# Batch 0 of a fused attention and FFN kernel: K projected twice, Q by chunk, FFN from single chunks, kv in two pieces, and a new written-out order

## Chip, cores, metric

One core of one Trainium2 chip. The metric is device microseconds (us) of one execution of the program. A core has TensorE (PE, matmul), VectorE (DVE), ScalarE (ACT), GpSimd (POOL) and SyncE (SP); each runs its own instruction queue in order and waits on semaphores. PE writes to PSUM, which has eight banks of 128 x 512 fp32 here. DVE and ACT take results out of the banks. DMAs are issued from the queues of SP, ACT and POOL.

## The reference

8 batches, 8 heads, 576 tokens, head size 64, 128 features. Linear attention with an exponential feature map, then a gated FFN (512 to 1536 to 512) over all 4608 tokens:

```
def phi(x):
    proj = np.einsum('bhsd,df->bhsf', x, w_phi)
    proj = proj - np.max(np.abs(proj), axis=-1, keepdims=True)
    return np.concatenate([np.exp(proj), np.exp(-proj)], axis=-1)
q_p, k_p = (phi(q), phi(k))
kv  = np.einsum('bhsf,bhsd->bhfd', k_p, v)
z   = np.sum(k_p, axis=2)
num = np.einsum('bhsf,bhfd->bhsd', q_p, kv)
den = np.einsum('bhsf,bhf->bhs', q_p, z)[..., None] + 1e-06
x   = (num / den) as rows of 8 heads x 64          # 4608 x 512
out = (np.maximum(x @ w_gate, 0.0) * (x @ w_val)) @ w_out
```

## The kernel before

The program is made of 1427 small steps ("atoms"), each a few instructions of one or two engines. The builder adds them with a key, and a string `ORDER` lists their numbers in the order in which their instructions enter the queues. A number with a prime takes the step's other engine (`copy_of`, line 276): a copy on DVE instead of ACT or the reverse, a scaling on DVE instead of POOL. `z3` and `z1` are matmuls of zeros that keep PE busy. Nothing else sets the order of the work; the queues wait on one another only where data or a buffer is needed. PSUM banks come from one pool of eight (line 172).

**K and V of a batch** (`k_atoms`, `k_item`). Batches 0 and 1 are handled in groups of 4 or 8 blocks of 128 tokens (`K_CUTS`; six groups in batch 0, of 4, 4, 8, 8, 8, 4 blocks, two heads sharing a block's 128 columns as two "parities"). For a group, PE turns K (`kT`, line 271), DVE or ACT copies it out (`kTc`, line 284), PE projects it with `w_phi` into two banks, one for each parity (`kr`, line 312). From these banks DVE takes the maximum of the absolute value (`km`, line 319) and ACT the two exponentials of projection and negated projection (`ke`, line 368). The maximum is not subtracted in the exponent: V's rows are scaled with its exponentials instead (`kk` on ACT, line 379, and `vs` on POOL, line 328). PE then sums K' times V (`kv`, lines 509 and 486), and the result is copied out (`kvc`, line 422). From batch 2 on, K and Q are turned by DMA transposes on SP (`turn`, lines 292 and 298), and tokens 512 to 575 of two batches together form "tails" (tiles km, vm, qm; a load of them is two DMAs, line 236).

**Q of a batch** (`q_item`), in two pairs of chunks; a chunk is 128 tokens. PE projects Q two ways: with features down the partitions (`qc`, line 549), for ACT's exponentials (`qe`, line 567), and with tokens down the partitions (`qr`, line 312), for DVE's maxima (`qm`, line 319). One step `qk` takes the exponentials of all maxima of a pair. Numerator and denominator come from PE (`n`, line 597) and are put together on DVE (`nt`, `nu`, lines 616 and 628, and the reciprocal, line 635); POOL divides (`xu`, line 642). In batches 0 and 1 PE turns the result (`xT`) and a copy writes it into the x of the batch (`xc`, line 662).

**FFN of a batch** (`ffn`). A step takes 128 of the 1536 hidden columns: four matmuls for the value (`fv`, line 734), copied out (line 749); four for the gate (`fg`), joined with the value on DVE (line 756). Then the output in thirds of the hidden columns (`fo`, line 791), copied out (line 805) and stored. Group 8 is the tails. In batch 0 the first four column blocks are done in halves of 256 tokens (`FIRST`, line 20), chunks 0 and 1, then 2 and 3, and the other eight over all 512 tokens.

**Loads.** V in fp32 and the K of batch 0 (fp32, in V's buffer `vn1`, which V of batch 1 takes next) go by SP; everything that is cast on the way (Q, other K, weights) goes by POOL. A small copy on POOL (`gate`, line 831) makes POOL's first load wait for a first piece of K. In the order before, SP's queue reads: loads of K and V of batch 0 (lines 812 to 823, ahead of the list), transposition of qm0 (position 100), V of batch 1 (151), transposition of K of batch 2 (227), and so on. POOL's loads are, in order: q0, k1, wv0, wg0, q1, wv1, qm0, wg1, wv2, wg2, k2, wo (a number after k, v, q is the batch; after wv and wg the third of the columns; after km, vm, qm the pair of batches).

Of the kernel before, what the change touches and what calls it, by code (L numbers as in the profile page):

```python
# [16 lines left out]

K_CUTS = [[4, 8, 16, 24, 32], [8, 16, 24, 32]]

FIRST = ((0, 2, 0, 4), (2, 4, 0, 4), (0, 4, 4, 12))  # L20
# [3 lines left out]


ORDER = """7 z3 82 92 93 83' 84 87 94 86 8 0 98 102 85 89 90 91 88 103 z1 104 96 97 108 105 95 107 106 z1 112
113 109 99 101 110' 111 122 114 115 123' 124 127 118 116 132 1 117 133 119 120 121 125 100' 128 z1
148 149 129 126 187 10 134 188 151 153 155 137 2 131 156 135 158 160 142 130 196 144 136 200 198
150 154 236 139 141 237 143 140 246 247 157 159 152 29 161 162 226 190 192 54 138 256 257 175 163
194 176 164 165 189 145 147' 191 266 177 146 3 267 193 4 169 170 166 167 171 168 195 199 181 178  # L30
182 321 214 5 172 179 183 180 184 201 197 217 215 11 220 221 218 222 219 208 9 322' 216 173 174'
282 283 223 209 185 186' 202 203 238 227' 210 205 206 204 207 240 211 1092 1093 1094 224 225' 239
1095 1096 324 328 228 229 242 212 213' 1097 326 232 1098 1099 1100 1101 1102' 231 6 1103 1104 1105
1106 1107 230 241 1108 243 268 269 270 271 273 258 274 272 261 248 251 260 249 253 255 254 1109 252
259 263 39 1110' 1111 1112' 264 1113 1114 275 250 233 1115 1116' 1117 290 361 262 363 265 292 365
279 280' 281' 323 327 291 295 293 1118 1119 294 1120' 1121 284 325 288 330 30 51 332 334 234 245
244 235 276 277 329 333 285 287 13 40 278' 289 1122 1123 351 296 1124 335 352 353 309 312 310 311
# [3 lines left out]
347' 32 55 61 371 372 307 308' 16 1134 63 388 398 402 399 391 400 383 385 1135' 1136 389 1137 401  # L41
42 403 1138' 405 393 367 368 369 395 392 394 390 1139 1140 1141 33 1142' 1143 1144' 17 43 424 426
428 384 418 454 458 420 1145 456 1146' 422 1147 1148 460 462 464 465 419 421 423 508 512 509 1149
# [4 lines left out]
502 1163 1164 1165' 534 536 538 564 529 531 523 1166 1167 568 503 570 476 574 566 533 569 571 1168  # L48
573 515 514 516 572 18 1169 1170 535 517 539 528 537 530 488 491 524 492 525 526 527 532 1171' 1172
# [70 lines left out]
def kernel(  # L120
# [161 lines left out]
    def turned_copy(st, n, by):  # L282
        st["T"] = sb_T.tile([P, n, P], BF16, name=f"tT{n}", bufs=3 if n == 4 else 2)
        copy_by(by)(st["T"].rearrange("p a b -> p (a b)"), st["pt"][:, 0 : n * P])

    for b in range(TURN, B):
        for n in "kq":

            @atoms.add("turn", n, b)
# [16 lines left out]
    def half_rows(par):  # L306
        return slice(D * par, D * (par + 1))
# [556 lines left out]
```

## Time and profile before

Three runs: 378.77, 378.97 and 380.34 us, median 378.97. One execution was profiled; its first to last instruction are the span. Its own time is not listed apart from the three.

| | |
|---|---|
| median of the runs | 378.97 us |
| span of the profiled execution | 377.4 us |
| PE / DVE / ACT / POOL busy | 98 / 77 / 56 / 40 % |
| granted clock of PE, mean | 0.995 |
| DMA bytes, mean rate | 45.10 MB, 120 GB/s |
| PE matmuls of the FFN, lines 734 and 791 | 1340 of 3502 |

How to read it: busy counts an instruction from start to end, and a matmul's end is modelled, so a busy PE need not be at its peak. Where PE has a steady gap between starts, the count of instructions by that gap is the work. "The chain of waits" follows back from the last instruction to whatever released each step; an engine's idle time matters only where this chain passes through it. A group of instructions carries its line, its engine, its operands as out<-in, shape, count, busy time and the mean of one. In the timeline, neighbours of one kind are merged, and a merged length runs from the first start to the last end. DMA rows give the size and the time from issue to landing. In the profile q0 is `qn`, K of batch 0 and V of batches 0 and 1 are `vn`, and qm0 is `qm`.

### The profile page before, as it was taken

The numbers are of one execution on the slowest core, as the hardware profiler recorded it, in microseconds if no ns is written. First come the engines' busy times: TensorE is split into PE (matmuls) and PEld (weight loads), VectorE is DVE, ScalarE is ACT, GpSimd is POOL, SyncE is SP. The second block draws the span as 40 slices with busy tenths as digits, with TensorE's granted clock in tenths as the row PEclk, the third lists the DMA queues.
The fourth block names the chain that finished last, engine by engine and source line by source line (L and its number), as shares of the span: only waits on it lengthen the run. The fifth ranks groups of instructions, "written<-read, shape, count | busy, mean of one in ns | idle before, by whom it ended". The sixth has DMA issues, their size and how long they took to land.

```text
span 377.4 us, 8960 instructions
## 1 busy us (share of the span) xinstructions
PE 368.1 (98%) x3502; PEld 197.4 (52%) x3502; DVE 290.7 (77%) x633; ACT 213.1 (56%) x509; POOL 151.3 (40%) x201
## 2 busy tenths in 40 slices
PE   7789999999999999999999999999999999999996
PEld 4568465546545555464554554465455444444443
DVE  6998999988876799888868886988768927824641
ACT  6997888877687556876765359882740302111101
POOL 5883672488275275901842126933700210000000
PEclk9899999999999999999999999999999999999999
DMA  8999999999489959781289678620410130021004
GB/s 260 205 200 215 233 131 174 219 172 137 89 213 236 165 67 171 144 182 28 59 160 179 96 174 132 130 16 16 128 41 2 29 113 29 2 67 58 2 2 109
DMA packets 87929, 45.10 MB, mean 120 GB/s; under 512 B 55824, under 2 KB 82000, under 8 KB 87888
## 3 DMA queue, kind: packets, MB, share of 16 engines
q1 hardware_dynamic: 60208, 30.42, 37.3%
q0 software_dynamic: 27200, 13.57, 28.8%
q8 instruction: 27, 0.44, 0.5%
q10 hardware_dynamic: 480, 0.56, 0.5%
q14 instruction: 14, 0.11, 0.1%
HBM read 37.78 MB, written 9.44 MB: 125 GB/s over the span
## 4 chain that ended last, share of the span: by engine, by line
PE 92%; ACT 3%; DMA 3%; issue 0%; SPq 0%; DVE 0%; POOL 0%; DVEq 0%
PE pa L734 49%; PE pa L791 25%; PE pa L597 5%; PE pa L312 5%; PE pa L486 4%; PE pa L549 2%; DMA qn<-in_q_dram 2%; ACT qp L567 2%; PE pa L271 1%; PE pa L509 1%; DMA vn<-in_k_dram 1%; ACT kp L368 1%; ACT kv L422 0%; ACT val_sb L749 0%; ACT xT L662 0%
## 5 line engine op out<-in xcount | busy, mean ns | idle before, releaser
L791 PE MATMUL pa<-wo_sb,h 128*128 128x512 bf16 (+2 forms) x444 | 99.9, 373 | 0.0
L734 PE MATMUL pa<-xT,wv_sb 128*128 128x512 bf16 (+1 forms) x400 | 99.3, 370 | 0.1
L734 PE MATMUL pa<-xT,wg_sb 128*128 128x512 bf16 (+1 forms) x400 | 99.3, 370 | 0.0
L756 DVE SCALAR_TENSOR_TENSOR h<-pa,val_sb 128x512 bf16<-128x512 f32 (+1 forms) x112 | 74.6, 669 | 27.2 <-PE pa L734 20.5
L749 ACT CAST val_sb<-pa 128x512 bf16<-128x512 f32 (+1 forms) x67 | 38.1, 575 | 97.1 <-PE pa L734 88.0
L567 ACT ACTIVATE qp<-pa 128x512 bf16<-128x512 f32 x144 | 76.2, 618 | 15.1 <-PE pa L549 14.8
L368 ACT ACTIVATE kp<-pa 128x512 bf16<-128x512 f32 (+1 forms) x152 | 77.4, 605 | 11.1 <-PE pa L312 9.8
L328 POOL TENSOR_TENSOR vs<-vn,ek 128x512 bf16<-128x512 f32 (+1 forms) x68 | 67.4, 1005 | 31.1 <-DMA vn<-in_v_dram 15.2
L734 PEld LDWEIGHTS <-wv_sb 128*128 128x128 bf16 x448 | 41.9, 98 | 44.9 <-issue 1.2
L734 PEld LDWEIGHTS <-wg_sb 128*128 128x128 bf16 x448 | 41.6, 98 | 43.5 <-issue 0.7
L791 PEld LDWEIGHTS <-h 128*128 128x128 bf16 x444 | 40.8, 98 | 44.6 <-issue 0.8
L319 DVE TENSOR_REDUCE mq<-pa 128x4 f32<-128x512 f32 x72 | 46.5, 683 | 10.4 <-PE pa L312 10.1
L319 DVE TENSOR_REDUCE mk<-pa 128x4 f32<-128x512 f32 (+1 forms) x76 | 47.8, 653 | 3.9 <-ACT kp L368 2.3
L642 POOL TENSOR_TENSOR xu<-u,r 128x512 bf16<-128x512 f32 x22 | 22.8, 1041 | 67.4 <-DVE r L635 53.5
L642 POOL TENSOR_TENSOR tT<-u,r 128x512 bf16<-128x512 f32 x14 | 14.6, 1042 | 73.0 <-DVE r L635 41.0
L628 DVE TENSOR_TENSOR u<-pa,t 128x195 f32<-128x195 f32 (+3 forms) x120 | 38.2, 333 | 3.3
L616 DVE TENSOR_TENSOR t<-pa,cq 128x195 f32<-128x195 f32 (+3 forms) x120 | 36.8, 325 | 2.2 <-PE pa L597 1.0
L597 PEld LDWEIGHTS <-qp 128*128 128x128 bf16 x640 | 28.1, 98 | 14.0 <-ACT qp L567 0.9
L749 DVE CAST val_sb<-pa 128x512 bf16<-128x512 f32 (+1 forms) x45 | 30.7, 682 | 4.5 <-PE pa L734 3.0
L597 PE MATMUL pa<-kv,qp 128*128 128x65 bf16 x640 | 31.0, 193 | 0.9 <-ACT qp L567 0.5
L805 DVE COPY out_sb<-pa 128x512 f32<-128x512 f32 x13 | 8.9, 688 | 13.8 <-PE pa L791 13.6
L486 PEld LDWEIGHTS <-kp 128*128 128x128 bf16 x480 | 16.6, 98 | 3.9 <-issue 0.7
(71 smaller groups left out, 278.4 us busy)
## 6 DMA issues: line engine op xcount, KB each, us to landing
vn<-in_v_dram SPq DMA_DIRECT2D x6, 1024.0 KB, 7.3
qn<-in_q_dram POOLq DMA_DIRECT2D x8, 512.0 KB, 8.6
out_dram<-tT SPq DMA_DIRECT2D x16, 256.0 KB, 2.9
out_dram<-out_sb SPq DMA_DIRECT2D x16, 256.0 KB, 2.9
kn<-in_k_dram POOLq DMA_DIRECT2D x6, 512.0 KB, 9.1
wv_sb<-in_moe_w_val_dram POOLq DMA_DIRECT2D x3, 512.0 KB, 10.2
wg_sb<-in_moe_w_gate_dram POOLq DMA_DIRECT2D x3, 512.0 KB, 9.1
wo_sb<-in_moe_w_out_dram POOLq DMA_DIRECT2D x1, 1536.0 KB, 19.5
```

The lines of the kernel that those rows point to most:

```text
L319: nc.vector.tensor_reduce(m, some.rearrange("p (c f) -> p c f", f=F), axis=AX.X, op=ALU.max, apply_absolute_value=True,)
L328: eng.tensor_tensor(dst[:, :, s, 0:D], src, ek[:, :, s : s + 1].to_broadcast(list(src.shape)), op=ALU.mult,)
L368: nc.scalar.activation(st["kp"][:, s, 0 : n // 2, par, :], st["banks"][par][:, 0 : n // 2 * F].rearrange("p (a f) -> p a f", f=F), AF.Exp, ...
L567: nc.scalar.activation(x["qp"][:, s, slot].rearrange("p a b -> p (a b)"), st["cols", i][par], AF.Exp, scale=sign,)
L597: nc.tensor.matmul(pn[:, E * (2 * i + s) : E * (2 * i + s + 1)], lhsT=x["qp"][:, s, slot, blk, :], rhs=kv_of(b, lo + i)[:, s, :],)
L616: nc.vector.tensor_tensor(x["t", j][rows, 0:n], ab[:, :, 1], c[:, :, None].to_broadcast([np_, n, E]), op=ALU.mult,)
L628: nc.vector.tensor_tensor(x["u"][rows, lo : lo + n], ab[:, :, 0], x["t", j][rows, 0:n], op=ALU.add)
L642: copy_of(alt, nc.gpsimd, nc.vector).tensor_tensor(x["xu"], x["u"][:, :, 0:D], x["r"].to_broadcast([P, H, D]), op=ALU.mult)
L734: nc.tensor.matmul(ps, lhsT=w[:, dc, P * fi : P * fi + P], rhs=xTs[g][:, dc, lo:hi], start=(dc == 0), stop=(dc == NDC - 1),)
L749: copy_by(copy_of(alt, "ACT", "DVE"))(st["val", n], ps)
L756: nc.vector.scalar_tensor_tensor(st["h2"][:, fi, lo:hi], ps, 0.0, st["val", n], op0=ALU.max, op1=ALU.mult)
L791: nc.tensor.matmul(po, lhsT=st["h2"][:, fi, P * t : P * t + P], rhs=wo_sb[:, fi, c0:c1], start=(fi == 0), stop=(fi == NFC - 1),)
```

## The change

It has five parts in code, all in batch 0, and a new `ORDER` of 1437 steps for the whole program.

1. *K twice.* For the six groups of batch 0 a new step `kx` repeats the projection into two further banks; the maxima are taken from these, the exponentials from the first two.
2. *Q by chunk.* For both pairs of batch 0, `qc`, `qr` and `qk` are split by parity, which here is the chunk: one bank and one chunk at a time.
3. *FFN in smaller token pieces.* `FIRST` becomes 128 tokens for column blocks 0 to 3 in chunk 0 and in chunk 1, 256 tokens for blocks 4 to 7 in chunks 0 and 1 and for 0 to 7 in chunks 2 and 3, and 512 for blocks 8 to 11. A piece of 128 tokens takes four column blocks into one bank, one of 256 tokens two, so every copy out is 512 wide; there are 12 value and 12 gate steps, where there were 16 and 16. Matmuls of batch 0's value and gate: 192, before 128.
4. *kv in two.* For both halves of batch 0, the matmuls of the last four of 18 blocks are a step of their own, after the rest.
5. The choice of two output buffers goes by index instead of by a running count.

There are also switches that are left off (`PLAIN` is empty, `Q_TURN` and `X_TURN` are 2 as `TURN` is).

```diff
-FIRST = ((0, 2, 0, 4), (2, 4, 0, 4), (0, 4, 4, 12))
+FIRST = ((0, 1, 0, 4), (1, 2, 0, 4), (0, 2, 4, 8), (2, 4, 0, 8), (0, 4, 8, 12))
+SPLIT = {(0, 0), (0, 1)}
+KV_LAST = {0: 4}
+TWICE = {(0, 0), (0, 1), (0, 2), (0, 3), (0, 4), (0, 5)}
...
-            st["banks"] = [bank(), bank()]
+            st["banks"] = {par: bank() for par in range(2)}
             rows_of(st["T"], st["banks"])
+        twice = key in TWICE
+        if twice:
+            @atoms.add("kx", *key)
+            def _(alt):
+                st["again"] = {par: bank() for par in range(2)}
+                rows_of(st["T"], st["again"])
...
-                row_max(st["m"][:, par:n:2], st["banks"][par][:, 0 : n // 2 * F])
+                row_max(st["m"][:, par:n:2], st["again" if twice else "banks"][par][:, 0 : n // 2 * F])
...
+        last = [x for x in order if x[2] >= 2 * CP * (part + 1) - KV_LAST.get(b, 0)]
+        order = [x for x in order if x not in last] + last
+        cuts = [0, len(order) - len(last), len(order)]
+        for piece, (lo, hi) in enumerate(zip(cuts, cuts[1:])):
...
+            for pars in ((0,), (1,)) if split else ((0, 1),):
+                at = (i, *pars) if split else (i,)
+                @atoms.add("qc", *key, *at)
...
+                @atoms.add("qr", *key, *at)
...
+        for ci in range(len(chunks) if split else 1):
+            @atoms.add("qk", *key, *((ci,) if split else ()))
...
+        def half_step(fi, nf, w, lo, hi):
+            ps = bank().rearrange("p (f n) -> p f n", f=nf)
+            for i in range(nf):
+                for dc in range(NDC):
+                    nc.tensor.matmul(
+                        ps[:, i],
+                        lhsT=w[:, dc, P * (fi + i) : P * (fi + i + 1)],
+                        rhs=xTs[g][:, dc, lo:hi],
```

The two order strings, written out by their keys (first number batch, then group or pair, and so on):

| queue | before | after |
|---|---|---|
| SP, after the loads of K0 and V0 | turn qm0 (100), v1 (151), turn k2 (227), turn km1 (265), turn q2 (279), turn k3, v2, vm1 | vm1 (64), v1 (143), turn qm0 (179), turn k2 (207), turn km1 (224), v2 (273), turn q2 (288), turn k3 (297) |
| POOL, loads | q0, k1, wv0, wg0, q1, wv1, qm0, wg1, wv2, wg2, k2, wo | qm0, q0, k1, wv0, q1, wv1, wg0, wg1, wv2, wg2, wo, k2, km1 |
| POOL, scalings of V0 | ten of twelve; two on DVE | all twelve, behind the first four loads |
| DVE, up to the first FFN step | maxima and copies of K0, Q0 and part of K1, two scalings of V0, mixed with the numerators of all four chunks | 17 steps of K0 (copies and maxima), then copy of Q, the last K maximum, copy of Q, eight Q maxima with two kv copies and three copies of turned K1, six products and six sums of the numerators of chunks 1 and 0, two reciprocals, the copy of chunk 1's x |
| PE, around Q0 | turning of Q pair 0 (56), of pair 1 (60), last K group (62) | turning of pair 1 (58), of pair 0 (59), kv part 0 (82, 91), last K group (90), kv part 1 (112, 113) |
| first FFN step | column block 0, chunks 0 and 1 (173) | column blocks 0 to 3, chunk 1 (166) |
| first output step of batch 0 | 286 | 302 |

The positions are those in the list. Behind batch 0 the steps are the same as before in another order; output thirds of one batch are mixed with value and gate steps more than before. The last steps of both lists are the last output tile's two parts of 352 and 160 columns.

More of the change, by code (lines that the diff above doesn't have):

```diff
@@ L284, in turned_copy @@
         copy_by(by)(st["T"].rearrange("p a b -> p (a b)"), st["pt"][:, 0 : n * P])
-    for b in range(TURN, B):
-        for n in "kq":
+    for b in range(min(TURN, Q_TURN), B):
+        for n, first in (("k", TURN), ("q", Q_TURN)):
+            if b < first:
+                continue
             @atoms.add("turn", n, b)
@@ L310, in rows_of @@
         for j in range(T.shape[1]):
-            for par in range(2):
+            for par in banks:
                 nc.tensor.matmul(
@@ L751, in _ @@
+        for n, (fi, nf, lo, hi) in enumerate(steps):
+            @atoms.add("fv", g, n)
+            def _(alt, n=n, fi=fi, nf=nf, lo=lo, hi=hi):
+                ps = half_step(fi, nf, wv_sb, lo, hi)
+                st["val", n] = sb_g.tile([P, SF], BF16, name="val_sb")
+                copy_by(copy_of(alt, "ACT", "DVE"))(
+                    st["val", n], ps.rearrange("p f n -> p (f n)")
+                )
             @atoms.add("fg", g, n)
-            def _(alt, n=n, fi=fi, lo=lo, hi=hi):
+            def _(alt, n=n, fi=fi, nf=nf, lo=lo, hi=hi):
```

269 lines of the change are left out of this document (151 added, 118 removed), and 38 rows, old and new, of the table ORDER.

## Prediction

> **What bounds the kernel now.** I read the page first, then the chain of waits in order of time, then busy time by windows, then the queues of SyncE (SP) and GpSimd (POOL).
>
> ```profile
> span 377.4 us, 8960 instructions
> PE 368.1 (98%) x3502; PEld 197.4 (52%) x3502; DVE 290.7 (77%) x633; ACT 213.1 (56%) x509; POOL 151.3 (40%) x201
> PE 92%; ACT 3%; DMA 3%; issue 0%; SPq 0%; DVE 0%; POOL 0%; DVEq 0%
> ```
>
> TensorE (PE) carries 92% of the chain that ended last; the other 8%, some 30 us, is where time can be won or lost. The chain in order of time (start, length, what) says where that is:
>
> ```profile
> 3.79 8.76 DMA qn<-in_q_dram
> 12.60 1.78 PE pa L271 x16
> ...
> 342.62 20.72 PE pa L734 x96
> ```
>
> 96 matmuls in 20.72 us are 0.216 us each, without a gap: late in the program PE works at its rate, and only the amount of work counts. At the start the chain hangs on the load of batch 0's Q (q0 below), which lands at 3.79 + 8.76 = 12.55. Busy time by windows:
>
> ```profile
> core 0: us, PE busy (x) PEld busy (x) DVE busy (x) ACT busy (x) POOL busy (x), PEclk, DMA share, GB/s
> 4.00:12.55 8.55, 6.54 (x51) 3.81 (x49) 6.77 (x13) 7.44 (x25) 5.98 (x11) 1.00 1.17 296
> 12.60:31.00 18.40, 16.60 (x338) 12.76 (x339) 17.63 (x52) 17.49 (x46) 15.90 (x22) 0.91 1.32 203
> 24.00:36.00 12.00, 11.21 (x153) 9.07 (x152) 10.85 (x37) 10.55 (x23) 6.96 (x8) 1.00 1.34 194
> 36.00:48.00 12.00, 12.00 (x124) 6.53 (x123) 10.92 (x20) 9.41 (x30) 6.75 (x11) 1.00 1.22 242
> ```
>
> From 36 us on PE is full (12.00 of 12.00). From 12.6 to 31, VectorE (DVE) and ScalarE (ACT) are full (17.63 and 17.49 of 18.40) and PE waits for them. So the time is the moment at which the FFN can begin to feed PE, plus the PE work that is then left. That moment is the first FFN matmul:
>
> ```profile
> 28.91 0.60 PE L734 MATMUL pa<-xT,wv_sb 128*128 128x256 bf16 x4
> ```
>
> It comes 28.91 - 12.55 = 16.4 us after q0 has landed. The change alters this distance, the landing of q0, and the work that is left.
>
> **Part 1: from q0 to the first FFN.** The new order starts the FFN on one 128-token chunk. I counted what DVE must do, in its new order, from q0's landing to that point: two copies of turned Q, one half-wide K maximum, eight Q maxima, two kv copies, three copies of turned K of batch 1, six products and six sums of the numerators, two reciprocals, one copy of turned x.
>
> ```profile
> L319 DVE TENSOR_REDUCE mq<-pa 128x4 f32<-128x512 f32 x72 | 46.5, 683 | 10.4 <-PE pa L312 10.1
> L662 DVE COPY xT<-pa 128x512 bf16<-128x512 bf16 x1 | 0.4, 427 | 0.2 <-PE pa L271 0.2
> ```
>
> ```profile
> 5.40 0.43 DVE L319 TENSOR_REDUCE mk<-pa 128x2 f32<-128x256 f32 x1 [0.23 <-ACT kp L368]
> 13.99 1.28 DVE L284 COPY tT<-pa 128x1024 bf16<-128x1024 bf16 x2
> 15.80 2.06 ACT L567 ACTIVATE qp<-pa 128x512 bf16<-128x512 f32 x4 [0.41 <-PE pa L549]
> 18.65 0.94 DVE L284 COPY tT<-pa 128x512 bf16<-128x512 bf16 x2
> 19.51 1.88 DVE L319 TENSOR_REDUCE mq<-pa 128x4 f32<-128x512 f32 x3
> 23.16 0.42 DVE L422 CAST kv<-pa 128x260 bf16<-128x260 f32 x1
> 25.09 0.20 DVE L635 RECIPROCAL r<-u 128x8 f32<-128x8 f32 x1
> 26.14 0.79 DVE L616 TENSOR_TENSOR t<-pa,cq 128x195 f32<-128x195 f32 x3
> ```
>
> One maximum lasts 0.683 and three in a row 1.88, so each further one adds (1.88 - 0.68)/2 = 0.60: neighbours overlap by 0.08. With that overlap taken off where it applies: Q copies 1.2; maxima 8 x 0.60 = 4.8, and 0.4 for the half-wide one; kv copies 0.7; K copies 3 x 0.43 = 1.3; twelve numerator steps at 0.79/3 = 0.26, 3.1; reciprocals and x copy 0.8. Sum 12.3. Ahead of it PE turns the first half of Q, half of the 1.78 above, 0.9. So the first FFN comes 13.2 us after q0, against 16.4: **-3.2**. ACT allows it: it has eight pairs of Q exponentials (2.06 for four, so 8.2 in all), two half-wide K pairs and five small steps, about 10.9 behind 2 us of turning and projecting. What makes the distance shorter is work that moves behind the first FFN: by position, 22 numerator matmuls with their DVE steps, and the second chunk's x.
>
> **Part 2: when q0 lands.** Here the order moves DMAs. On POOL, the Q tails of batches 0 and 1 (qm0) are now issued ahead of q0. On SP, batch 0's loads were followed by the transposition of qm0, and batch 1's V (v1) stood behind that. SP's waits and its timeline:
>
> ```profile
> SPq L298 <- DMA qm<-in_q_dram: 23.6, 1, 23.6
> ```
>
> ```profile
> 27.71 1.30 SPq L298 DMA_TRANSPOSE qmT<-qm  x1
> 29.26 0.40 SPq L220 DMA_DIRECT2D vn<-in_v_dram  x1
> ```
>
> SP stood 23.6 us at that one wait, so v1 left at 29.26, although the buffer that it takes (K of batch 0 was in it) was free once PE had turned the last of K0. That was at 11.6:
>
> ```profile
> 3.79 1.07 POOL L214 DMA_DIRECT2D qn<-in_q_dram  x1
> 11.19 0.44 PE L271 MATMUL pa<-ident,vn 128*128 128x128 f32 x2
> 21.24 1.42 POOL L236 DMA_DIRECT2D qm<-in_q_dram  x2
> ```
>
> In the new order SP's queue holds vm1 (V tails of batches 2 and 3), v1, and only then the transposition. vm1 has nothing to wait for and leaves at about 4; v1 leaves after that last turning, near 11. An engine goes by its own queue, not by the position in the list: SP waited from 4 us on, at position 100. So both loads meet q0.
>
> ```profile
> vn<-in_v_dram SPq DMA_DIRECT2D x1, 1152.0 KB, 11.5
> vm<-in_v_dram SPq DMA_DIRECT2D x6, 128.0 KB, 8.4
> qm<-in_q_dram POOLq DMA_DIRECT2D x8, 64.0 KB, 4.1
> ```
>
> ```profile
> 36.00:41.00 5.00, 5.00 (x49) 3.07 (x47) 4.54 (x10) 4.13 (x15) 0.06 (x1) 1.00 1.22 297
> 41.00:46.00 5.00, 5.00 (x25) 2.25 (x23) 4.66 (x8) 3.40 (x12) 4.69 (x8) 1.00 1.24 205
> ```
>
> Bounds for q0: at the least only qm0 is ahead of it, 128 KB at the 203 GB/s that POOL's loads reach by themselves, +0.65: 13.2. At the most vm1 (256 KB) and v1 (1152 KB) pass q0 too, 1.44 MB at the 296 GB/s of that stretch, +4.9 more: 18.1. v1 landed 11.5 after its issue, so at 40.8; while it ran, in 36 to 41, everything together moved 297 GB/s, against 205 after it. 1.18 MB at 297 are 4.0. v1 starts near 12, and by then q0, behind qm0, has hardly begun; most of v1 passes it. I take 17.0, near the upper end, **+4.4**.
>
> The Trainium skill (DMA: Bandwidth & Descriptors, section Where 436 GB/s comes from) gives about 358 GB/s for loads from HBM. By that the 1.44 MB would cost 4.0, an estimate from that page, and the sum would be up to 0.9 lower; the windows here show less than 300, and I stay with them.
>
> Nothing covers this wait. In DVE's queue seventeen steps of K0 stand ahead of the first Q copy, done near 13; behind it stands all of Part 1. In PE's queue the turning of Q stands ahead of the last K group's projection and of kv. POOL could become late as well, since all twelve V scalings are now its own and start 1.42 later:
>
> ```profile
> L328 POOL TENSOR_TENSOR vs<-vn,ek 128x512 bf16<-128x512 f32 (+1 forms) x68 | 67.4, 1005 | 31.1 <-DMA vn<-in_v_dram 15.2 <-ACT ek L379 11.5 <-ACT pa L409 2.6
> ```
>
> 12 x 1.0 and a load's issue from 8 us on end at 21 to 22; kv wants the last of them some 5 us after q0, at 22. That costs nothing with q0 at 17.0, and up to 3 with q0 at 13.2.
>
> First FFN: 17.0 + 13.2 = 30.2, **+1.3**.
>
> **Part 3: PE work that is left then.** It grows, since Part 1 put some of it off. From the chain in order of time:
>
> ```profile
> 34.86 3.64 PE pa L734 x28
> 57.65 0.81 PE pa L597 x26
> 69.35 0.45 PE pa L271 x8
> 84.64 0.78 PE pa L312 x24
> ```
>
> 22 numerators x 0.031 = 0.7, eight turnings (x and K1) 0.45, eight projections of K1 0.26: +1.4. FFN pieces: 64 more matmuls in batch 0. The 28 in 3.64 are 24 of 256 columns and 4 full ones; (3.64 - 4 x 0.216)/24 = 0.116 against half of 0.216, so 0.008 each more: +0.4 to +0.5. The second projection of K, 36 x 0.0325 = 1.2, lies ahead of the first FFN, where PE waits for DVE; without that cover it would cost its 1.2. Fewer and wider copies out of the FFN's banks spare DVE and ACT some 0.6 each, but behind PE: nothing. kv in two pieces adds no matmul. wo's load now stands ahead of K of batch 2, priced at nothing as long as its transposition is done before PE's queue comes to it. Part 3: **+1.8**.
>
> What the second projection buys is small:
>
> ```profile
> DVE mk L319 <- ACT kp L368: 0.2, 1, 0.2
> ```
>
> In the first 36 us DVE waited 0.2 us for ACT on a shared bank. The Trainium skill (PSUM — Partial Sum Buffer, section PSUM bank collisions raise a hardware error) says that two engines must not read one bank at once, so that schedulers order them. By that rule each K maximum stands against its exponentials, and separate banks should win more than 0.2; here other steps of DVE fill those gaps, and the sum by the trace stays.
>
> **Sum**: +1.3 (which is +4.4 - 3.2, with rounding) + 1.8 = +3.1: span 380.5. The median of the three runs, 378.97, lies 1.6 above the span, and I hold that fixed. **Forecast 382.1.**
>
> **The rivals.**
> *The loads do not collide*: v1 shares little, or leaves late. q0 at 13.4, first FFN 26.6: -2.3 + 1.8, so 378.5, no change. For it: q0 was being served when v1 would start. Against it: v1's buffer was free at 11.6 already.
> *Faster*: q0 at 13.2, first FFN 26.4 (-2.5); the 0.8 us that PE lacked in 24 to 36 goes as well, because single chunks reach it more evenly, and of the 1.8 some 1.0 is done there: 376.5. It decides if q0 lands before 13.4 and POOL is in time. Against it: DVE and ACT, full already, have no room.
> *Weights late*: POOL's loads are a queue at 203 GB/s until 31 us, so all slide with q0: K1 19.9, then 2.6 each, Q1 25.1, the third value block 35.5. The transposition of qm0 now shares with them; past 2.5 us of that, the turning of Q1 and the FFN wait: +2.5, 384.6.
> *The second projection does not do what it is for*: that is inside the forecast, 1.2 of PE's waiting time for at most 0.2.
>
> **How the numbers follow.** Collision 0.55, no collision 0.23, faster 0.12, late weights 0.10. A measurement here tells 0.5%, 1.9 us, from no change: faster is below 377.1, slower above 380.9. The collision case goes from q0 at 15.5 (380.6) to 18.1 (383.2), so a tenth of it is no change; a tenth of the second is faster. Faster 0.14, same 0.27, slower 0.59. Range 377.2 to 384.6.
>
> **What would show it.** Right: v1 leaves SP near 11; q0 lands at 16 or later; DVE is idle 3 to 4 us before the first copy of turned Q; the first FFN is near 30 and PE full from about 36. Wrong: q0 before 14.5 (Part 2 fails), more than 14.5 us from q0 to the first FFN (Part 1 fails), or gaps of PE after 40 us, which a new order could hold anywhere and which no row of before can show.

## The result, and the profile after

The changed kernel takes 390.02 us (median of four runs, 388.79 to 393.09) against 379.31 (four runs, 378.77 to 380.34): ratio 1.029, interval 1.0245 to 1.0335, 10.7 us slower. Ratios here and below are of fast executions alone; of the experiments' executions one was slow (392.68 us, before with K0 projected twice). The profiled execution took 389.5. The forecast, 382.1, had the direction; the time lies 5.4 us above the end of its range.

Of the page of the changed kernel: the span, the busy times, the granted clock in 40 slices, and the shares of the chain.

```profile
span 387.7 us, 9067 instructions
PE 372.0 (96%) x3550; PEld 205.9 (53%) x3602; DVE 292.3 (75%) x637; ACT 221.1 (57%) x521; POOL 139.5 (36%) x182
PEclk9788999999999999999999999999999999999999
PE 84%; DMA 6%; DVE 5%; issue 2%; ACT 1%; POOL 0%; SPq 0%; DVEq 0%
```

PE's share of the chain fell from 92% to 84%; transfers, DVE and "issue" took it. 52 matmul records are missing (3550 of 3602, up to five in any 20 us), so gaps of 0.1 to 0.2 us in the PE rows are not evidence here. I use the weight loads (PEld), which are complete. Lines have moved: turning 290, projection by rows 333, numerators 675, value and gate 814, output 875, loads 233 to 271.

The chain of the changed kernel in order of time (start, length, what):

```profile
3.81 1.47 POOL qm L255 x2
5.29 10.20 DMA qn<-in_q_dram
...
15.54 1.90 PE pa L290 x16
...
17.73 11.04 DMA qn<-in_q_dram
...
28.82 2.53 PE pa L290 x22
```

q0 lands at 5.29 + 10.20 = 15.49. The chain then does not go through the steps of DVE, as forecast, but through a second load, that of batch 1's Q (q1). It leaves at 17.73 and lands at 28.77. POOL's timeline says why it leaves then, the DMA rows of the kernel before say what the same load took there, and PE's timeline says when the FFN begins:

```profile
17.73 0.94 POOL L233 DMA_DIRECT2D qn<-in_q_dram  x1 [3.35 <-PE pa L290]
```

```profile
qn<-in_q_dram POOLq DMA_DIRECT2D x1, 512.0 KB, 8.5
```

```profile
32.27 0.94 PE L814 MATMUL pa<-xT,wv_sb 128*128 128x128 bf16 x14
```

q1 takes q0's buffer, so POOL waited 3.35 us until PE had turned q0. The load then took 11.04 us against 8.5. The turning of Q1 (positions 144 and 149) stands ahead of the first FFN step (166) in PE's queue. So the first FFN step comes at 32.27, 16.8 us after q0, 3.4 later than before.

This is one execution. Four of the experiments below have the same loads up to q1, and their profiles show how much q0 varies:

| kernel | q0 lands | q1 lands | first FFN step |
|---|---|---|---|
| after | 15.49 | 28.77 | 32.27 |
| Q1's turning late | 15.37 | 28.23 | 28.86 |
| after, then the later order of before | 16.84 | 29.35 | 31.65 |
| K once | 17.09 | 28.94 | 32.24 |
| V2 late | 18.43 | 29.44 | 32.91 |

With q0 at 16.84 or later the chain runs through q0's load and the steps behind it, as forecast, though more through PE's and ACT's than through DVE's, and the first FFN step comes 14.4 to 15.1 us after PE begins to turn q0. With q0 at 15.49 it runs through q1. The two paths are nearly equally long, and the first FFN step stays between 31.65 and 32.91 unless Q1's turning is moved.

On SP:

```profile
4.07 1.55 SPq L255 DMA_DIRECT2D vm<-in_v_dram  x2
12.03 0.39 SPq L239 DMA_DIRECT2D vn<-in_v_dram  x1
```

The two loads of V left about when the forecast said (4 and near 11). Busy time by windows (columns as in the prediction):

```profile
10.00:20.00 10.00, 7.59 (x87) 5.38 (x86) 7.19 (x14) 6.69 (x19) 6.63 (x11) 0.75 1.30 233
20.00:30.00 10.00, 8.76 (x221) 7.10 (x218) 8.55 (x25) 8.11 (x22) 8.76 (x13) 0.84 1.31 204
30.00:40.00 10.00, 10.00 (x166) 8.92 (x166) 7.84 (x23) 7.20 (x14) 5.54 (x7) 0.89 1.24 207
```

DVE and ACT, full before, are now busy 6.7 to 8.6 of 10. PE's granted clock is 0.75 to 0.89 in these windows; before it is 0.83 from 10 to 20 us and 1.00 from there on. This shows on the path: from 28.8 to 31.3 us the granted clock is 0.50, and the 22 turnings behind q1's landing (last line of the chain above) take 0.115 us each, where eight in the kernel before took 0.45, 0.056 each. So some 1.3 us of the 3.4 are the clock's in this execution.

**Where the 10.3 us of span went.** Take the start of each step's first weight load and subtract the PE work that the list has put ahead of it, each matmul at its duration by shape (0.216 us for 512 columns, 0.031 for a numerator, 0.0325 for a projection, and so on). What remains is the time that PE has lost so far, to waits, to a lower clock and to anything else between its instructions. In us, at seven times (the lower four kernels are experiments, below); next to a long stop a figure can be 1.5 off, since it hangs on the step that is read:

| kernel | 38 | 58 | 70 | 100 | 160 | 290 | 340 | PE work |
|---|---|---|---|---|---|---|---|---|
| before | 14.2 | 14.7 | 15.1 | 15.9 | 17.7 | 20.3 | 20.4 | 355.6 |
| after | 17.5 | 18.1 | 19.7 | 21.6 | 25.0 | 29.4 | 29.5 | 356.7 |
| before, then the later order of after | 14.4 | 15.2 | 15.6 | 17.3 | 20.3 | 24.5 | 24.6 | 355.6 |
| after, early loads as before | 11.6 | 18.8 | 19.9 | 21.7 | 24.9 | 29.4 | 29.4 | 356.7 |
| before, early loads as after | 21.2 | 21.9 | 22.3 | 23.3 | 24.8 | 28.0 | 27.9 | 355.6 |
| before, K0 projected twice | 15.6 | 16.3 | 16.8 | 17.7 | 19.3 | 22.1 | 22.2 | 356.6 |

After less before: 3.4 us up to 58 us, 1.1 of added work, 1.2 more between 58 and 70, and 4.5 spread over all that follows. Together 10.2. More than half of the loss comes behind the place at which the forecast stopped looking for gaps.

Between 58 and 70 there is one stop, 1.4 us at 63.7 (timeline of the changed kernel):

```profile
63.59 0.25 ACT L661 ACTIVATE cq<-mq 128x8 f32<-128x8 f32 x1
65.15 0.38 PE L675 MATMUL pa<-kv,qp 128*128 128x65 bf16 x7 [1.41 <-issue]
65.38 0.56 DVE L694 TENSOR_TENSOR t<-pa,cq 128x130 f32<-128x130 f32 x2 [2.12 <-PE pa L675]
65.62 1.09 ACT L641 ACTIVATE qp<-pa 128x512 bf16<-128x512 f32 x2 [1.78 <-PE pa L675]
```

DVE and ACT wait for PE, and PE for nothing that the profile names ("issue").

### The profile page after: what moved, and what is told of

Its sections match the earlier page's. It is cut to its first block, busy times and chain, and to the rows that moved or that the text cites. A ratio compares the mean times of both kernels' runs of the same rounds, so it can differ in the third digit from the quotient of the medians.

```text
span 387.7 us, 9067 instructions
## 1 busy us (share of the span) xinstructions
PE 372.0 (96%) x3550; PEld 205.9 (53%) x3602; DVE 292.3 (75%) x637; ACT 221.1 (57%) x521; POOL 139.5 (36%) x182
## 4 chain that ended last, share of the span: by engine, by line
PE 84%; DMA 6%; DVE 5%; issue 2%; ACT 1%; POOL 0%; SPq 0%; DVEq 0%
PE pa L814 47%; PE pa L875 21%; DMA qn<-in_q_dram 5%; PE pa L675 5%; PE pa L333 4%; PE pa L548 4%; PE pa L622 2%; PE pa L290 2%; DVE h L838 1%; DVE tT L719 1%; DVE mk L340 1%; DVE t L694 1%; DVE u L706 1%; DMA vn<-in_k_dram 1%; PE pa L580 1%
## 5 line engine op out<-in xcount | busy, mean ns | idle before, releaser
L838 DVE SCALAR_TENSOR_TENSOR h<-pa,val_sb 128x512 bf16<-128x512 f32 x108 | 73.5, 688 | 35.0 <-PE pa L814 33.6
L814 PE MATMUL pa<-xT,wv_sb 128*128 128x512 bf16 (+2 forms) x421 | 93.9, 355 | 0.6
L814 PE MATMUL pa<-xT,wg_sb 128*128 128x512 bf16 (+2 forms) x414 | 92.0, 354 | 1.3 <-ACT qp L641 0.2
L829 ACT CAST val_sb<-pa 128x512 bf16<-128x512 f32 x71 | 41.6, 588 | 87.1 <-PE pa L814 75.9
L349 POOL TENSOR_TENSOR vs<-vn,ek 128x512 bf16<-128x512 f32 (+1 forms) x65 | 65.5, 1017 | 68.0 <-ACT ek L429 56.0
L415 ACT ACTIVATE kp<-pa 128x512 bf16<-128x512 f32 (+1 forms) x152 | 77.0, 590 | 15.9 <-PE pa L333 11.9
L641 ACT ACTIVATE qp<-pa 128x512 bf16<-128x512 f32 x144 | 76.4, 609 | 15.7 <-PE pa L622 13.7
L706 DVE TENSOR_TENSOR u<-pa,t 128x195 f32<-128x195 f32 (+3 forms) x120 | 37.2, 331 | 1.6 <-POOL tT L719 0.2
L719 POOL TENSOR_TENSOR xu<-u,r 128x512 bf16<-128x512 f32 x18 | 19.7, 1100 | 51.8 <-DVE r L713 17.8
L675 PE MATMUL pa<-kv,qp 128*128 128x65 bf16 x640 | 33.0, 194 | 2.2 <-issue 1.4
L829 DVE CAST val_sb<-pa 128x512 bf16<-128x512 f32 x37 | 25.4, 688 | 11.6 <-PE pa L814 11.2
L719 POOL TENSOR_TENSOR tT<-u,r 128x512 bf16<-128x512 f32 x8 | 8.3, 1040 | 42.6 <-DVE r L713 42.6
L889 ACT COPY out_sb<-pa 128x512 f32<-128x512 f32 (+1 forms) x12 | 6.9, 577 | 19.0 <-PE pa L875 19.0
## 6 DMA issues: line engine op xcount, KB each, us to landing
kn<-in_k_dram POOLq DMA_DIRECT2D x6, 512.0 KB, 10.3
```

The lines of the kernel that those rows point to most:

```text
L349: eng.tensor_tensor(dst[:, :, s, 0:D], src, ek[:, :, s : s + 1].to_broadcast(list(src.shape)), op=ALU.mult,)
L415: nc.scalar.activation(st["kp"][:, s, 0 : n // 2, par, :], st["banks"][par][:, 0 : n // 2 * F].rearrange("p (a f) -> p a f", f=F), AF.Exp, ...
L641: nc.scalar.activation(x["qp"][:, s, slot].rearrange("p a b -> p (a b)"), st["cols", i, par], AF.Exp, scale=sign,)
L675: nc.tensor.matmul(pn[:, E * (2 * i + s) : E * (2 * i + s + 1)], lhsT=x["qp"][:, s, slot, blk, :], rhs=kv_of(b, lo + i)[:, s, :],)
L706: nc.vector.tensor_tensor(x["u"][rows, lo : lo + n], ab[:, :, 0], x["t", j][rows, 0:n], op=ALU.add)
L814: nc.tensor.matmul(ps[:, i], lhsT=w[:, dc, P * (fi + i) : P * (fi + i + 1)], rhs=xTs[g][:, dc, lo:hi], start=(dc == 0), stop=(dc == NDC - 1),)
```

## The experiments

In the diffs below a line is a place in the list, by key; where a step changes its function, the code is shown. Each ratio is against runs of the kernel before on the same chip (medians 379.3 to 379.9).

### The two halves of the list

```diff
 ORDER of after, places 0 to 299
-ORDER of after, places 300 to 1440
+the steps that are left, in the order of before
```

> The changed kernel with its own order for the first 300 places (batch 0, the first group of the FFN's steps, up to about 58 us) and, behind them, the order of the kernel before for all that is left. Theory: the loss has two parts. By the weight loads of TensorE, the changed kernel is 3.6 us behind before at 58 us, has 1.1 us more TensorE work, and loses another 5.5 us between 58 us and the end. So this kernel should lose the first two alone: 379.3 + 4.7 = 384 us. Rival: the whole loss comes from the start (late loads, a late first FFN step), and what is lost later follows from it: 389 to 390 us, as the changed kernel.

Measured: 386.38 us, ratio 1.0153 (1.006 to 1.0246, a wide interval: 2.3 to 9.3 us).

```diff
 ORDER of before, places 0 to 283
-ORDER of before, places 284 to 1430
+the steps that are left, in the order of after
```

> The kernel before with its own first 284 places and, behind them, the changed kernel's order for all that is left. K is projected once, Q whole, the FFN by 512 hidden columns, as before. Theory of two parts: it loses only what the later order costs, 379.3 + 5.5 = 385 us, with first FFN step at 29 us as before. Rival, all of the loss from the start: 379 us, within 1 us of before.

Measured: 383.46 us, ratio 1.009 (1.0056 to 1.0125). The two medians add up: +6.7 and +3.8 against +10.7 for both. The rival (all from the start) falls by the second kernel, whose interval excludes no change. My split was 1.5 to 2.4 us off: the start costs more, the later order less. PE's waits from 28 us on, in the second kernel:

```profile
PE pa L734 <- ACT qp L567: 0.2, 1, 0.2
PE pa L734 <- DVE h L756: 0.2, 1, 0.2
PE pa L597 <- DVE mk L319: 0.2, 1, 0.2
PE pa L312 <- DVE kv L422: 0.2, 1, 0.2
```

The same view of before has no line from 36 us on. No single wait makes the later order's loss: by the table it grows from 0.5 us at 70 to 4.2 at 290. What the waits show is 0.8; the rest is spread over steps too short for that view, and its cause stays open. It is not a larger number of changes between matmuls of 64 and of 128 rows: between 70 and 340 us there are 56 of them in before and 57 in this kernel.

### What sets the start: V late, Q1's turning late

```diff
-ld vm1 (64)
-ld v1 (143)
 turn qm0 (179)
+ld vm1
+ld v1
```

> The changed kernel with the two loads of V that left early on SP (the tail rows at 4.07 us, batch 1 at 12.03 us) put back behind the transposition of Q's tail rows, as before. Theory: they share the DMA engines with the loads of Q for batches 0 and 1, which land at 15.49 and 28.77 us; without them q0 lands 1 to 2 us earlier and q1 3 us earlier, the first FFN step comes at 29 to 30 us instead of 32.4, and the time falls by 2 to 3 us, to 387 to 388. Rival: POOL's queue alone sets when q0 and q1 land (qm ahead of q0; K of batch 1 and a third of W_val ahead of q1): they land where they did, 390 us.

Measured: 389.41 us, ratio 1.0235 (1.015 to 1.0319). Its chain:

```profile
5.29 8.94 DMA qn<-in_q_dram
...
16.47 12.67 DMA qn<-in_q_dram
```

q0 lands 1.3 us earlier as expected, but q1 takes 12.67 us and lands at 29.14, as late as ever. The transposition comes early in this kernel too, so V1 left at 14.62, only 2.6 us later, and met q1 instead of q0. Inconclusive for the collision.

```diff
-qT 1 0 (144), qT 1 1 (149), qTc 1 0 (155), qTc 1 1 (161)
 fg 0 0 4 0 1 (202)
+qT 1 0, qTc 1 0, qT 1 1, qTc 1 1
```

> The changed kernel with the two turnings of batch 1's Q and their copies put behind the first six FFN steps in the order, so that TensorE does not wait for q1 (28.77 us) ahead of the first FFN step. Theory: the first FFN step comes 13 to 14 us after q0, at 29 us, and about 2 us of the 3.5 us lost at the start are won back: 388 us. Rival: the first FFN step waits for its own operand (the normalised and turned rows of batch 0) nearly as long as for q1, or the wait turns up again at Q1's projection: within 0.5 us of 390.

Measured: 390.69 us, ratio 1.0265 (1.0177 to 1.0352). In its trace PE turns q0 at 15.41 and the first FFN step comes at 28.86, 13.45 us later: with Q1 out of PE's way the distance is close to the forecast 13.2. Yet nothing is gained. The stop near 63 us is 2.3 us long instead of 1.4, and PE waits elsewhere:

```profile
PE pa L675 <- issue: 2.3, 1, 2.3
PE pa L675 <- DVE mk L340: 0.8, 1, 0.8
...
PE pa L814 <- ACT kp L415: 0.6, 1, 0.6
```

### A buffer of its own for q1

```diff
+def load_q1(b, name, src, eng, dtype):
+    t = sb_in.tile([P, H * C // 2, P], dtype, name="qT1").rearrange("p a b -> p (a b)")
 ...
 ld q0 (24)
+ld q1
 ld k1 (31)
...
-ld q1 (75)
```

> The changed kernel with a buffer of its own for batch 1's Q (the one that batch 3's turned Q takes much later), and its load directly behind batch 0's Q on POOL, instead of at 17.73 us after TensorE has turned batch 0's Q. Theory: batch 1's Q lands near 20 to 21 us instead of 28.77, TensorE no longer stands before its turning, the first FFN step comes 13 to 14 us after q0, at 29 to 30 us instead of 32.4, and, since Q1's own work is not put off as in the kernel with the late turning, the 3 us are kept: 387 us. Rival: the projections and the V scalings of batch 1 are set by K1 and the weights, which now land later; the first FFN step moves little and the time is 389.5 to 391.

Measured: 392.18 us, ratio 1.0338 (1.0297 to 1.0379), the slowest of all by its median. The rival holds: the wait only changes its name. K of batch 1 is now the load that takes long, and the turning of K1 also stands ahead of the first FFN step, which comes at 34.28. From its chain:

```profile
7.75 17.91 DMA kn<-in_k_dram
...
25.70 1.03 PE pa L295 x8
```

### The loads alone, both ways

```diff
 ld wv1 (98)
+ld qm0
...
 turn qm0 (179)
+ld vm1, ld v1
...
 turn k3 (297)
+ld v2
```

> The changed kernel with the order of its loads put back to that of before in four places: Q's tail rows behind the second third of W_val on POOL, the tail rows and batch 1 of V behind the transposition of Q's tail rows on SP, batch 2 of V behind the transposition of batch 3's K. Theory: q0 lands at 12.5 to 13.5 us instead of 15.49 and q1 at 25 to 26 instead of 28.77; first FFN step near 29; the stop of TensorE at 63.7 us goes as well; together 3 + 1.5 us less: 385 to 386 us. What then is left over before (6 us) is the second projection of K, about 1.1 us of TensorE work, and the later order, 3.8 us. Rival: the loads are hidden and the order of the compute steps alone makes the start late: q0 lands earlier but the first FFN step stays at 32 us, 389 to 390 us.

Measured: 388.47 us, ratio 1.0235 (1.0206 to 1.0263), not the 385 to 386 expected. In this kernel PE turns q0 at 12.86 and the first FFN step comes at 26.30, 13.44 us later and 2.6 us earlier than in before. By the table PE has lost 11.6 us at 38 us: 2.6 less than before, 5.9 less than after. Nearly all of it goes again, in one wait of 4.8 us and behind it (from 56.5 to 63.3 us the granted clock is 0.50):

```profile
PE pa L580 <- POOL vs L349: 4.8, 1, 4.8
```

```profile
vn<-in_v_dram SPq DMA_DIRECT2D x1, 1152.0 KB, 18.7
```

V of batch 1, issued at 29.76 with W_out, K2 and Q2 on their way, needs 18.7 us to land; POOL's scalings start at 48.65, and the kv matmuls of batch 1 stand in PE's queue for them. Now the converse, before's compute order with after's loads:

```diff
+ld qm0
 ld q0 (0)
...
+ld vm1, ld v1
 turn qm0 (100)
```

> The kernel before with only its early loads ordered as the change orders them: Q's tail rows ahead of batch 0's Q on POOL, the tail rows and batch 1 of V ahead of the transposition of Q's tail rows on SP. Theory (the forecast's own term): q0 lands at 14 to 17 us instead of 12.55 and the first FFN step as much later; 381 to 383 us. Rival: it lands later, but VectorE and ScalarE use the time for batch 0's K, so that less than half of it stays: 379.5 to 380.5.

Measured: 386.55 us, ratio 1.0183 (1.0158 to 1.0208): **6.9 us for three moved loads**, more than twice what I expected. Its chain and its largest PE wait:

```profile
5.29 10.31 DMA qn<-in_q_dram
15.64 1.90 PE pa L271 x16
17.83 14.12 DMA qn<-in_q_dram
31.99 0.72 PE pa L271 x8
```

```profile
PE pa L271 <- DMA qn<-in_q_dram: 4.1, 1, 4.1
```

q0 is 3 us late; q1, whose buffer q0 holds, leaves 2.5 us later than in before and then takes 14.12 us instead of 8.5.

The leaving matters less than it seems. In the five kernels of the table above and in the one with V late, q1 leaves anywhere between 16.47 and 20.66 and lands between 28.23 and 29.44. An estimate by the bytes ahead of q1 fits better: the three loads are 1536 KB, which at the 204 GB/s of 20 to 30 us in the changed kernel are 7.7 us, and q1 lands 8.2 later than in before (31.95 against 23.75). In the changed kernel the first third of W_gate, 512 KB, stands behind q1 and not ahead of it; the 1024 KB that are left are 5.1 us, and q1 lands 5.0 later. One of the three loads by itself:

```diff
+ld v1
 turn qm0 (100)
...
-ld v1 (151)
```

> The kernel before with one load moved: V of batch 1 stands on SP ahead of the transposition of Q's tail rows, so it leaves near 11 to 12 us instead of 29.26. Q's tail rows stay late on POOL, V's tail rows stay late too. Theory: of the 6.9 us that the changed order of the loads costs on the kernel before, this one megabyte is the larger part: it passes the end of q0's load and the loads in front of batch 1's Q; q0 lands 0.5 to 1.5 us later, q1 at 28 to 30 us instead of 24; 383 to 385 us. Rival: Q's tail rows ahead of q0 are the part that counts, since they put off every later load of POOL's queue, and V1 alone costs 0 to 1 us.

Measured: 382.58 us, ratio 1.0077 (1.0048 to 1.0105). V1 alone costs 3.3 us, just below the theory's range and not the rival's 0 to 1. Its chain goes through q1, which is issued at 15.27 (in before at 15.28) and takes 12.26 us; it lands 3.8 later, where the estimate by bytes would say 5.8:

```profile
15.27 12.26 DMA qn<-in_q_dram
27.58 1.03 PE pa L271 x8
```

If the loads' costs add, the other half, 3.6 us, belongs to Q's and V's tail rows, which were not run by themselves.

### The stop at 63.7 us

```diff
-ld v2 (273)
 turn q2 (288)
 turn k3 (297)
+ld v2
```

> The changed kernel with one load moved: V of batch 2 (1 MB, issued on SP at 56.30 us ahead of the transposition of batch 2's Q) stands behind the transposition of batch 3's K, as in the kernel before. In the changed kernel TensorE stops for 1.4 us at 63.7 us, with nothing that the profile names; the one transfer that ends then is a 16 KB packet of the instruction queue (62.91 to 63.87 us), asked for some 4 us late by the count of TensorE's instructions, while 16 DMA engines were full; the kernels with late V or late turning stop there too (1.4 and 2.3 us). Theory: TensorE ran out of instructions, because the packet stood behind the crowd of V2, K3 and the transposition of Q2; with V2 out of the way it comes near 59 to 60 us, the stop goes, and the time falls by 1.4 to 2 us, to 388 to 388.6. Rival: the stop is a wait for a buffer or a bank that the profile does not name; it stays, 390 us.

Measured: 388.21 us, ratio 1.022 (1.0189 to 1.025), 1.8 us less by the medians; the intervals just touch. PE's waits after 28 us for which the profile names nothing, first of the changed kernel, then of this one, in which the stop is gone:

```profile
PE pa L675 <- issue: 1.4, 1, 1.4
PE pa L875 <- issue: 0.5, 3, 0.2
```

```profile
PE pa L875 <- issue: 0.5, 3, 0.2
```

The page of the changed kernel has a queue for instructions (packets, MB, share):

```profile
q8 instruction: 28, 0.46, 0.5%
```

28 packets of 16 KB for some 7200 instructions of PE (3602 weight loads and as many matmuls) are one for every 256. In the changed kernel the sixth runs from 62.91 to 63.87 us, and PE goes on at 65.15. Count PE's instructions up to the moment this packet has landed, in all kernels with the changed start:

| kernel | landed at | instructions issued by then | stop of PE |
|---|---|---|---|
| after | 63.87 | 1720 | 1.4 |
| V late | 64.85 | 1720 | 1.4 |
| Q1's turning late | 63.46 | 1720 | 2.3 |
| after, then the later order of before | 63.65 | 1720 | 2.2 |
| start kept, below | 60.98 | 1720 | 2.0 |
| own buffer for q1 | 64.87 | 1698 | 0.3 |
| V2 late | 63.01 | 1686 | none |
| K once, below | 64.66 | 1670 | none |
| early loads as before | 60.43 | 1570 | none |
| first of "Can the early start be kept?" | 61.90 | 1670 | none |
| the same, K once | 63.25 | 1632 | none |
| start kept, K once | 61.54 | 1668 | none |

PE stops at exactly 1720 wherever the packet comes later than that, and, but for 0.3 us in one kernel, not where it comes earlier. Instruction 1721 is issued 1.3 to 1.6 us after the landing in all five, and 1.4 after it with the own buffer for q1 and with V2 late, which is why the first of these still stops for 0.3. It is not the step itself, a numerator in every kernel of the table: it passes without a stop where the packet is early. So PE has run out of instructions. Late in the changed kernel the packets leave at 6526, 6792 and 7038 instructions issued, about 256 apart; by that spacing the sixth was due near 1410, and left at 1700. Two things meet there. PE takes instructions fast: it issues number 1406 at 58.7 us and number 1662 at 60.7. And the packet left 4.2 us after number 1406. With V2 out of the way it left 2.7 us after it and landed at 63.01, not at 59 to 60 as expected. That fits a packet held up by the data transfers, of which V2 was a part; what else holds it was not tested. In two of these kernels the view of waits names DVE for the stop ("DVE u L706: 2.2" and "2.0"): DVE had been done, and its semaphore was only the last event seen. The Trainium skill (Runtime: NRT & Kernel Launch, section Instruction fetch mechanics) says that instructions come in 16 KiB blocks through a DMA queue that the sequencer drives, and that the cost is mostly hidden. The block size agrees; here it was not hidden, at 1.4 to 2.3 us.

### The second projection of K

```diff
-TWICE = {(0, 0), (0, 1), (0, 2), (0, 3), (0, 4), (0, 5)}
+TWICE = set()
-kr 0 u, kx 0 u
+kr 0 u, where the first of the two stood
```

> The changed kernel with K of batch 0 projected once, the maxima and the exponentials read from the same banks as before the change; all else, the order too, as changed (a projection stands where the first of its two stood). Theory: the second projection is 36 matmul pairs, 1.2 us of TensorE work in a stretch in which TensorE waits for q0 and q1 anyway: the time falls by 0 to 0.5 us, 389.5 to 390. Rival A: the work is on the path, 388.8. Rival B: with one bank the exponentials of ScalarE and the maxima of VectorE get into each other's way (banks come free later), and the time rises by 0.5 to 1 us.

Measured: 386.49 us, ratio 1.0184 (1.015 to 1.0217), 3.5 us less than after. 1.0 is PE work and 1.4 the stop (the list is 72 instructions shorter, so PE reaches the limit after the packet, as the table shows); about 1 us more is not accounted for. The theory (0 to 0.5 us) falls; it is rival A, the work is on the path, and more. The converse:

```diff
+        if key[0] == 0:
+            @atoms.add("kx", *key)
+            def _(alt):
+                st["again"] = [bank(), bank()]
+                rows_of(st["T"], st["again"])
...
 kr 0 u
+kx 0 u
```

> The kernel before with only the second projection of batch 0's K added, directly behind the first, the maxima read from its banks. Theory: 36 more pairs of 0.033 us, 1.2 us, in a stretch where TensorE waits, and four banks of eight taken at once: 0 to 1 us slower, 379.5 to 380.7. Rival A: VectorE and ScalarE no longer wait for each other at a bank, and the time falls by 0.5 us. Rival B: banks run short ahead of the first FFN step and the time rises by 2 us or more, which would put most of the start's loss on the second projection.

Measured: 381.74 us, ratio 1.0053 (1.0032 to 1.0074): 2 us slower. In its trace PE turns q0 at 13.74 and the first FFN step comes at 31.17, 17.4 us later, where before has 16.3. (That q0 is turned 1.1 later than in before is within what q0 varies as POOL's first load, 12.5 to 13.7.) DVE's waits for PE's projections up to 33 us, first of before, which has one such line, then of this kernel (with its waits for turned tiles, 1.5 us in before):

```profile
DVE mk L319 <- PE pa L312: 0.4, 1, 0.4
```

```profile
DVE mq L319 <- PE pa L312: 2.0, 1, 2.0
DVE tT L284 <- PE pa L271: 1.8, 2, 0.9
DVE mk L319 <- PE pa L312: 1.2, 2, 0.8
```

The maxima now wait for PE, 3.2 us in all against 0.4; the doubled projections stand in PE's queue ahead of what DVE needs next. PE "waiting for DVE" was not free room.

### Can the early start be kept?

```diff
 places 0 to 299 of after, then the order of before
 ld q1
+ld qm0
 turn qm0
+ld v1
 turn k3
+ld v2, ld vm1
```

> The changed kernel's first 300 places with four loads moved (Q's tail rows directly behind batch 1's Q on POOL; batch 1 of V behind the transposition of Q's tail rows; batch 2 of V and the tail rows of V behind the transposition of batch 3's K), and the order of the kernel before for all the rest. In the kernel with the loads as before, TensorE was at 51.9 us 5.7 us ahead of the changed kernel (first FFN step at 26.5 us) and lost it again in one wait of 4.8 us for POOL's scaling of batch 1's V, whose load took 18.7 us to land behind W_out and K2. Theory: with V1 on its way some 5 us earlier that wait goes; first FFN step at 26.5 to 28 us, no stop of TensorE near 63 us, the later order as before: 1 to 2 us faster than before, 377.5 to 379 us. Rival: V1 in flight with Q1 makes Q1 late again, first FFN step at 30 us or later, 380 to 382.

Measured: 384.74 us, ratio 1.0125 (1.0096 to 1.0153). That is neither the theory's 377.5 to 379 nor the rival's 380 to 382: the first FFN step comes at 27.30, but with V1 earlier the weights are late. Chain and waits:

```profile
23.92 17.20 DMA wv_sb<-in_moe_w_val_dram
41.17 6.99 PE pa L814 x36
```

```profile
PE pa L814 <- DMA wv_sb<-in_moe_w_val_dram: 2.6, 1, 2.6
```

The same with one projection of K (`TWICE = set()`, `kr` where the first of the two stood):

> The same, with K of batch 0 projected once, maxima and exponentials read from the same banks. Theory: the 1.0 us of TensorE work of the second projection lies in stretches in which TensorE waits for Q, and only the part that does not costs: within 0.5 us of the kernel with both. Rival A: it is on the path, as the 3.5 us between the changed kernel and the one with a single projection suggest (of which 1.8 us were the stop for instructions): 1 us faster. Rival B: the second set of banks pays, and a single projection is 0.5 to 1 us slower.

Measured: 383.62 us, ratio 1.0108 (1.0085 to 1.0131); 1.1 less, with intervals that overlap.

```diff
 places 0 to 299 of after, then the order of before
 ld wv1
+ld qm0
 turn qm0
+ld v1
 vs 1 0 1 (243)
+ld wo
 vs 1 2 0 (274)
+ld km1, turn km1
 vs 1 4 0 (283)
+ld q2
 turn k3
+ld v2, ld vm1
```

> The changed kernel's first 300 places, the order of before for all the rest, and the loads in this order: Q's tail rows behind the second third of W_val, batch 1 of V behind their transposition, and W_out, K's tail rows and batch 2 of Q only behind scalings of batch 1's V, so that V1 has the DMA engines nearly to itself; batch 2 of V and V's tail rows behind the transposition of batch 3's K. Theory: with the loads as before TensorE was 2.1 us ahead of the kernel before at 52 us, net of the 1.1 us of the second projection about 1 us, and only V1 was late (18.7 us to land, behind W_out, K2, K's tail rows and Q2). With those four out of its way it lands by 40 us, the scalings end before TensorE needs them, and the lead is kept: 378 to 379 us, 0.2 to 0.4% faster than before. Rival: the loads of the first 50 us fill the DMA engines whatever their order; what is put off (W_out, Q2) is then late at its own place near 60 us, and the time is 381 us or more.

Measured: 384.06 us, ratio 1.012 (1.0087 to 1.0153). V1 is in time now, and PE has lost 12.8 us at 38 us, but then:

```profile
PE pa L675 <- DVE u L706: 2.0, 1, 2.0
PE pa L814 <- DMA wg_sb<-in_moe_w_gate_dram: 0.8, 1, 0.8
...
PE pa L875 <- DMA wo_sb<-in_moe_w_out_dram: 0.6, 1, 0.6
```

The weights are late again, W_out (put off) is late at the first output step, and the first line is the stop for instructions.

And this one with one projection of K:

> The same with K of batch 0 projected once. Theory: the second projection costs 1 to 2 us when the loads do not hide it (2.1 us on the kernel before), so this one is 1 us faster than with it: 377 to 378. Rival: the second pair of banks is what lets the maxima and the exponentials run side by side in this order, and a single projection gives the lead away: 379 or more.

Measured: 384.36 us, ratio 1.0131 (1.0103 to 1.0158), not to be told from the one before.

So the times of the rivals of the last two expectations hold; the last one's reason, that the second pair of banks pays, is not shown, since both kernels take the same time. In each of the three orders of loads that let the FFN begin between 26.3 and 28.1 us, something else came late: V1, the weights, W_out, or instructions. No version beat the kernel before.

## Why the prediction failed

The direction was right, for part of the right reason; the size was not. By its own steps:

- **Part 1, "the first FFN comes 13.2 us after q0": wrong for this kernel, right as a count.** It was 16.8, and 14.4 to 15.1 in three other kernels with the same loads. With Q1's turning moved it was 13.45, with before's loads 13.44. The count went through DVE's and ACT's queues and left out what stands ahead in PE's: the turning of Q1, for whose load PE waited. In the three others the chain passes PE's and ACT's steps: with V2 late, of the 14.3 us from 18.47 to 32.73, PE has 7.5, ACT 5.0 and DVE, on whose steps the 13.2 was counted, 1.6.
- **Part 2, q0 at 17.0: 15.49 in the profile, but 15.4 to 18.4 over five kernels with the same loads.** So this number is not refuted; whether one execution hits it is luck. V1 left at 12.03 and vm1 at 4.07, near what was said, and DVE stood idle for 2.3 us before its first copy of Q, not 3 to 4. But the price of the collision was put on q0 alone, and q1 pays it as well: 28.77 against 23.75 in before. First FFN 32.27 instead of 30.2. Alone on before the moved loads cost 6.9 us and PE has lost 7.0 more at 38 us; in the changed kernel it has lost 3.3 more. That the first third of W_gate stands behind q1 there is one reason by the bytes; it was not run by itself.
- **Rival "weights late"** had the place: "the turning of Q1 and the FFN wait". It took Q1 to land at 25.1; it was 28.77. It should have been the forecast.
- **Part 3, the second projection "lies ahead of the first FFN, where PE waits for DVE"**: this failed. Alone it costs 2 us, of which 1.0 is the work itself.
- **"kv in two pieces adds no matmul", the FFN's 0.4, and wo ahead of k2 at nothing**: not run by themselves. Of the 1.1 us of added work in the table 1.0 is the second projection's, so the FFN's pieces add 0.1; no PE wait in the changed kernel names kv's copies or K2 for more than 0.2 us.
- **The step that cost most: everything behind 36 us was priced as PE work without gaps.** The forecast named such gaps among what would make it wrong, and gave them no case and no price. They are the later order, 3.8 us, spread over waits too short to name, and the stop for instructions, 1.4 to 1.8.

The forecast's +3.1 held 1.3 for the start and 1.8 for work. Measured: 3.4 to 58 us, 1.1 of work, 1.2 around the stop, 4.5 behind it.

## What to carry to other kernels

Where the DMA engines are full, a load that leaves early does not just use an idle queue: ask which load the engine that matters needs next, and how many bytes are then ahead of it. Count the distance to a step in every in-order queue that it passes, PE's own first. And a new order of a program whose main engine was full has a price of its own: run the list's halves against each other before explaining the parts.

## What was not expected of the hardware

- PE can run out of instructions in the middle of a program: 1.4 to 2.3 us in five kernels. In the changed kernel it came where PE used up 256 instructions in 2.0 us and the packet that it needed left 4.2 us after it was due by the later spacing.
- The same load at the same place took very different times: q0, issued at 5.3 to 6.0 us behind qm0, landed between 14.2 and 18.4 us in eight profiled kernels; where it was POOL's first load it landed between 12.5 and 13.7.
- The granted clock was 0.75, 0.84 and 0.89 in the three windows from 10 to 40 us, though PE was busy all the time in the last of them; before it was 1.00 from 20 us on.
